# A two-dimensional spectral filter: stage 1 of the first transform in two row tiles of 64 partitions

## The chip, the cores and the metric

The kernel runs on one core of a Trainium2 chip. A core has TensorE (PE, the matrix unit, with its weight loads written as PEld), VectorE (DVE), ScalarE (ACT), GpSimd (POOL) and SyncE (SP), which here only issues transfers, and sixteen DMA engines that all queues share. The metric is the device time of one execution in microseconds. Lower is better.

## The reference

The input x has 2048 rows and 1024 columns in bf16. Two filters, A and B, are applied to the same x, and a gate per row mixes the results:

```
g = sigmoid((x * gate_w).sum(-1, keepdims=True))
a = irfft2(rfft2(x) * (A_w_r + 1j*A_w_i))
b = irfft2(rfft2(x) * (B_w_r + 1j*B_w_i))
out = g * a + (1 - g) * b
```

The filters have 2048 by 513 complex weights each, in bf16. The output is 2048 by 1024 in bf16.

## The kernel before, in words

The transforms are written as matmuls with constant matrices, in seven stages, and the filters' product stands in the middle.

**Stage 1** takes the first part of the transform over the rows. x lies in WB with partition = 4 n1 + 2 b + dh: n1 counts blocks of 64 rows, b says which half of the block a row lies in, and dh is the left or the right half of a row's 1024 columns. The free dimension of WB has 32 rows of 512 columns. They are handled in eight groups c of four rows. The constant M (tile XR) has 64 columns for each of the 32 rows, of which 32 belong to b = 0 and 32 to b = 1; a partition has zeros in the columns of the other half. For each group, `prep` (token pp, line 426) writes a copy with the columns reversed into a zone of XR, `mvariant` (mv, line 417) writes three copies of M with signs, and `stage1` (s1, line 444) makes, for each of two column halves j, a job of eight matmuls: four rows q, once with x and once with the reversed copy, accumulating in PSUM. Each has 128 columns of x as weights and 256 columns of M and its variants as moving data. Group 6 (`FOLDED`) is treated differently: `prep` forms the sum and the difference of x and its reversed copy, and the job has eight matmuls of 128 columns. `evict1` (e1, line 467) copies the PSUM unit into FT. A few matmuls without use (`IDLE`, line 447) stand ahead of two jobs, and eleven of 512 columns at the very start.

**Stage 2** (s2, evicted by e2) takes the transform over the columns, **stage 4** (s4, e4) the second part over the rows. Both come in sixteen units, eight of the columns' set M and eight of set O. POOL swaps real and imaginary parts by transfers from XR to XR (sw). VectorE multiplies with the filters' weights W in tile WA: D with the direct data, S with the swapped ones, each in a quarter q and a half, written for instance D.M.1.1. W comes by `wload` in four groups for set M (("W", "M", 0) to 3) and two for set O (token wo).

**Stage 5** (s5, e5) begins the way back over the rows: 32 units of sixteen matmuls, units 16 to 31 of set M and 0 to 15 of set O. A unit of set O needs all products of that set. **Stages 6 and 7** (s6, e6; s7) end it; ad and cq combine and SP stores the rows.

The **gate** has its own chain: gs and egs take x's spectrum with the gate's weights, `row_sums` (rows) forms partial sums, zp sums them over the partitions on TensorE, ez copies the sums on ScalarE and lets POOL write them to gate_rows in DRAM, and zl lets SP read them back as two broadcasts, the first half of the rows into FT and the second into F2. sg applies the sigmoid on ScalarE (sg.0 the first, sg.1 the second), gm the sign on VectorE, and rb multiplies the result with the constant U5, whose two halves come by the tokens U5 and U5b on SP, behind zl. rb.0 to rb.7 use the first half of U5 and the rows, rb.8 to rb.15 the second. A unit s6.r needs rb.r.

**The order** is written out in `PLAN`, a table of tokens. Each token puts its instructions on its engine in the order of the table, and every engine works in order. The letter or word at the end of a token names the engine (a, d, pe, dma), the number before pe the PSUM unit, of which there are four with two banks each. `Prog` adds the waits that the data need. Transfers on SP go out in the order of the program too: first M and x, then F2 and CK, the W groups of set M with small constants between them, wo.0 and wo.1, the constant tail CL of CK, the gate's broadcasts, U5, DI and U5b, and the stores. A few x transfers are issued by ScalarE.

```
    for c in range(1, 8):
        xload(c, 0, "sp")
        xload(c, 1, "act" if c < 4 else "sp")
```

Of the kernel before, what the change touches and what calls it, by code (L numbers as in the profile page):

```python
# [22 lines left out]
def make_consts():  # L23
# [3 lines left out]
    n1, pb, dh = p // 4, (p // 2) % 2, p % 2  # L27
    M = np.zeros((128, 32, 16, 2, 2))
    for b in range(2):
        on = 1.0 * (pb == b)[:, None]  # L30
        n = 64 * n1[:, None] + 32 * b + np.arange(32)[None, :]
        for t in range(16):
            if t == 0:
                M[:, :, 0, 0, b] = on
                M[:, :, 0, 1, b] = on * ((-1.0) ** n1)[:, None]
            else:
                ph = pi2 * t * n / 2048
                M[:, :, t, 0, b] = on * np.cos(ph)
                M[:, :, t, 1, b] = -on * np.sin(ph)
    C["M"] = M.reshape(128, 2048)  # L40
# [58 lines left out]
    blocks += [np.ones((128, 128))]  # L99
# [60 lines left out]
D.M.0.1..d sw.M.0..dma gw.0.pe s2.M.5.2.pe e4.M.3..a D.M.0.0..d s2.M.4.1.pe egw..a sw.M.1..dma e2.M.5..a  # L160
gs.1.3.pe e2.M.4..a D.M.1.1..d s4.M.5.0.pe egs.1..a s4.M.4.2.pe D.M.1.0..d e4.M.5..a gs.3.1.pe e4.M.4..a
s2.M.7.3.pe S.M.0.1..d egs.3..a s2.O.1.0.pe e2.M.7..a S.M.0.0..d gs.2.2.pe e2.O.1..a S.M.1.1..d s4.M.7.1.pe
sw.M.2..dma egs.2..a s2.M.6.3.pe S.M.1.0..d e4.M.7..a gs.0.0.pe e2.M.6..a D.M.2.1..d s2.O.0.2.pe egs.0..a
D.M.2.0..d s4.M.6.1.pe e2.O.0..a s4.O.1.3.pe rows..d e4.M.6..a s4.O.0.0.pe e4.O.1..a sw.M.3..dma S.M.2.1..d
s2.O.3.2.pe e4.O.0..a s2.O.2.1.pe S.M.2.0..d wo.0..spq e2.O.3..a st.3.pe s2.O.5.0.pe D.O.0.0..d est..a
sw.O.0..dma e2.O.2..a s4.O.3.2.pe D.M.3.0..d e2.O.5..a s4.O.2.3.pe e4.O.3..a D.M.3.1..d s2.O.4.1.pe e4.O.2..a
# [782 lines left out]
```

## Time and profile before

| what | us |
|---|---|
| median of 3 runs | 122.81 (121.64 to 122.82) |
| the profiled execution | 122.8 |
| its span, from the first to the last instruction | 121.0 |
| TensorE busy | 113.5 |
| ScalarE busy | 103.5 |
| VectorE busy | 85.8 |
| GpSimd busy | 17.3 |

The times further down are from the profiled execution and count from the start of its span. In the views a line number such as L463 is a line of the kernel; L326, L329 and L332 are the helpers for transfers and copies, so their groups are told apart by their tiles. L601 is stage 5, L494 stage 2, L509 stage 4, L539 the products, L708 stage 6, L732 stage 7. "SPq" is a transfer being issued by SP; the time until its data land stands in another view. Matmuls overlap in their records, so the cost of one in a row is read from the length of a run of them.

### The profile page before, as it was taken

The numbers are of one execution on the slowest core, as the hardware profiler recorded it, in microseconds if no ns is written. First come the engines' busy times: TensorE is split into PE (matmuls) and PEld (weight loads), VectorE is DVE, ScalarE is ACT, GpSimd is POOL, SyncE is SP. The second block draws the span as 40 slices with busy tenths as digits, with TensorE's granted clock in tenths as the row PEclk, the third lists the DMA queues.
The fourth block names the chain that finished last, engine by engine and source line by source line (L and its number), as shares of the span: only waits on it lengthen the run. The fifth ranks groups of instructions, "written<-read, shape, count | busy, mean of one in ns | idle before, by whom it ended". The sixth has DMA issues, their size and how long they took to land.

```text
span 121.0 us, 3622 instructions
## 1 busy us (share of the span) xinstructions
PE 113.5 (94%) x1546; PEld 99.1 (82%) x1546; DVE 85.8 (71%) x127; ACT 103.5 (86%) x127; POOL 17.3 (14%) x37
## 2 busy tenths in 40 slices
PE   6979999999999999789999989999899999999990
PEld 2358899969689787488799989999899989999980
DVE  0375667319679969999979917999503879787772
ACT  0498999699878999979999989999979688988861
POOL 4000009306003393030530000000000000000000
PEclk9999999999999999999999999999999999999998
DMA  2999999999999999649893999300000334443344
GB/s 61 296 331 370 348 360 332 321 319 344 371 350 325 353 306 256 185 108 277 152 371 117 297 381 418 122 0 5 0 0 5 126 134 173 176 175 119 146 175 173
DMA packets 27519, 26.87 MB, mean 222 GB/s; under 512 B 10208, under 2 KB 23216, under 8 KB 27248
## 3 DMA queue, kind: packets, MB, share of 16 engines
q1 hardware_dynamic: 24368, 20.85, 55.8%
q0 software_dynamic: 1760, 4.49, 10.2%
q10 hardware_dynamic: 1376, 1.31, 3.5%
q8 instruction: 12, 0.20, 0.7%
q14 instruction: 3, 0.02, 0.1%
HBM read 18.23 MB, written 4.20 MB: 185 GB/s over the span
## 4 chain that ended last, share of the span: by engine, by line
PE 42%; DVE 17%; DMA 16%; ACT 12%; issue 5%; SPq 4%; POOL 0%; DVEq 0%; ACTq 0%; POOLq 0%
PE PS L732 11%; PE PS L708 10%; PE PS L463 10%; DMA XR<-XR 10%; ACT WB L329 9%; DVE WA L539 9%; DVE WB L539 5%; PE PS L601 5%; SPq L326 4%; DMA WA<-in_B_w_i_dram 4%; PE PS L494 3%; DMA SM<-c_SM 3%; ACT XR L329 2%; ACT WA L329 2%; DVE WA L776 1%
## 5 line engine op out<-in xcount | busy, mean ns | idle before, releaser
L601 PE MATMUL PS<-CK,WA 128*128 128x128 bf16 x256 | 31.8, 223 | 1.6 <-DVE WA L539 1.6
L601 PEld LDWEIGHTS PS<-CK,WA 128*128 128x128 bf16 x256 | 31.3, 145 | 1.9 <-DVE WA L539 1.9
L329 ACT ACTIVATE XR<-PS 128x1024 bf16<-128x1024 f32 x31 | 29.5, 1035 | 2.9 <-PE PS L494 1.6
L329 ACT ACTIVATE WB<-PS 128x1024 bf16<-128x1024 f32 (+1 forms) x31 | 30.8, 1040 | 1.4 <-PE PS L601 1.2
L601 PE MATMUL PS<-CK,WB 128*128 128x128 bf16 x256 | 31.9, 226 | 0.0
L601 PEld LDWEIGHTS PS<-CK,WB 128*128 128x128 bf16 x256 | 31.3, 145 | 0.1
L329 ACT ACTIVATE WA<-PS 128x1024 bf16<-128x1024 f32 (+5 forms) x34 | 25.3, 807 | 5.5 <-PE PS L708 2.8
L776 DVE TENSOR_TENSOR WA<-PS,WA 128x512 bf16<-128x512 f32 (+1 forms) x30 | 19.7, 711 | 10.7 <-ACT WA L329 10.5
L539 DVE TENSOR_TENSOR WB<-XR,WA 128x2048 bf16<-128x2048 bf16 x16 | 19.1, 1222 | 3.3 <-ACT XR L329 2.6
L539 DVE TENSOR_TENSOR WA<-XR,WA 128x2048 bf16<-128x2048 bf16 x16 | 18.7, 1224 | 2.9 <-DMA XR<-XR 2.8
L732 PE MATMUL PS<-FT,WA 128*128 128x256 bf16 x140 | 17.6, 273 | 0.2 <-ACT WA L329 0.2
L494 PE MATMUL PS<-F,FT 128*128 128x128 bf16 x256 | 16.0, 219 | 0.0
L494 PEld LDWEIGHTS PS<-F,FT 128*128 128x128 bf16 x256 | 14.8, 98 | 0.9
L509 PE MATMUL PS<-XR,CK 128*128 128x512 bf16 (+1 forms) x72 | 15.3, 355 | 0.0
L732 PEld LDWEIGHTS PS<-FT,WA 128*128 128x128 bf16 x140 | 13.1, 98 | 1.6 <-ACT WA L329 0.4
L708 PE MATMUL PS<-XR,WB 128*128 128x128 bf16 x208 | 13.6, 219 | 0.5 <-ACT WB L329 0.4
L708 PEld LDWEIGHTS PS<-XR,WB 128*128 128x128 bf16 x208 | 12.5, 98 | 1.0 <-ACT WB L329 0.8
L329 ACT ACTIVATE FT<-PS 128x1024 bf16<-128x1024 f32 (+1 forms) x14 | 12.4, 988 | 0.3 <-PE PS L463 0.3
L326 POOL DMA_DIRECT2D XR<-XR x16 | 8.4, 529 | 25.1 <-DVE WA L539 12.5
L509 PEld LDWEIGHTS PS<-XR,CK 128*128 128x128 bf16 x72 | 6.5, 97 | 5.1 <-ACT XR L329 0.2
L463 PE MATMUL PS<-XR,WB 128*128 128x256 bf16 x56 | 8.4, 273 | 0.9 <-DMA WB<-in_A_x_dram 0.6
L463 PE MATMUL PS<-XR 128*128 128x256 bf16 x56 | 8.4, 273 | 0.2 <-DVE XR L332 0.2
(74 smaller groups left out, 88.1 us busy)
## 6 DMA issues: line engine op xcount, KB each, us to landing
XR<-XR POOLq DMA_DIRECT2D x16, 256.0 KB, 4.9
out_dram<-WA SPq DMA_DIRECT2D x15, 256.0 KB, 2.0
WB<-in_A_x_dram SPq DMA_DIRECT2D x12, 256.0 KB, 6.9
FT<-c_U SPq DMA_DIRECT2D x2, 1024.0 KB, 9.6
WA<-in_A_w_r_dram SPq DMA_DIRECT2D x7, 192.5 KB, 4.9
WA<-in_A_w_i_dram SPq DMA_DIRECT2D x7, 192.5 KB, 5.0
WA<-in_B_w_r_dram SPq DMA_DIRECT2D x7, 192.5 KB, 5.0
WA<-in_B_w_i_dram SPq DMA_DIRECT2D x7, 192.5 KB, 5.9
```

What stands on the lines that cost most here:

```text
L326: return P.add(eng, lambda e: e.dma_start(dst, src), dma=name, **kw)
L329: return P.add("act", lambda e: e.activation(dst, src, ACT.Copy), **kw)
L463: P.add("pe", lambda e, o=ps(u * 1024 + q * 256, [(1, 256)]), lh=lh, rh=rh, s=s, q=q: e.matmul(o, lh, rh, start=(s == 0 and q % 2 == 0), s ...
L494: P.add("pe", lambda e, o=o, lh=fblock(cmb, j, t), j=j, rh=rh, cmb=cmb: e.matmul(o, lh, rh, start=(j == 0 and cmb == 0), stop=(j == 1), sk ...
L509: P.add("pe", lambda e, o=o, fb=FB[kind, pm, m], m=m, rh=rh: e.matmul(o, sl(CK, fb, [(1, 128)]), rh, start=(m == 0), stop=(m == 1)), r=["C ...
L539: pop[st, q, sw, half] = P.add("dve", lambda e: e.tensor_tensor(out=o, in0=x, in1=w, op=ALU.mult), r=xr(o_, 2048) + wk, a=[("prod", st, sw ...
L601: P.add("pe", lambda e, o=o, lh=sl(t, to + l0, [(hp, 128)]), ab=ab: e.matmul(o, lh, KI(ab), start=(ab == 0), stop=(ab == 1)), r=[("prod", ...
L708: P.add("pe", lambda e, o=o, lh=lh, rh=rh, cp=cp: e.matmul(o, lh, rh, start=(cp == 0), stop=(cp == 1)), r=[("Z", pi), ("RB", r)], w=[("ps" ...
L732: P.add("pe", lambda e, lh=lh, rh=rh, st=st, sp=sp: e.matmul(ps(bank * 512 + o, [(1, 256)]), lh, rh, start=st, stop=sp), r=[("Y", r), "DI" ...
L776: P.add("dve", lambda e, s=s, op=op: e.tensor_tensor(out=sl(WA, outc(r) + 512 * s, [(1, n), (2, 256)]), in0=ps(2 * u * 512, [(256, n), (1, ...
```

## The change

Stage 1 computes the same sums with another layout. The partition of x becomes 64 b + 2 n1 + dh, so each row half b has 64 neighbouring partitions. M loses the zeros and half of its columns. A job now has sixteen matmuls, each on 64 partitions and 128 moving columns; the two row halves write two different banks of the unit. No group is folded. M comes in three pieces instead of four, and `mvariant` works on a whole piece. x comes in seven pieces of four rows (one of eight), each by four transfers to 32 partitions, 28 in all instead of 16 to 64 partitions; five are issued by ScalarE and 23 by SP. FT's layout between stages 1 and 2 changes with it (`evict1`, `fblock`). The zones are eight instead of four. The scratch tile VT of `row_sums` is dropped for the tail of CK, so the transfer CL, which fills that tail, now comes after `row_sums`; a block of ones in CK that nothing reads is dropped. The table `PLAN` is written anew as a whole, so the order of the products, evictions, stage-5 units, rb and the gate's tokens changes too.

```diff
@@ make_consts
-    n1, pb, dh = p // 4, (p // 2) % 2, p % 2
-    M = np.zeros((128, 32, 16, 2, 2))
...
-    C["M"] = M.reshape(128, 2048)
+    n1, pb, dh = p // 2 % 32, p // 64, p % 2
+    M = np.zeros((128, 32, 16, 2))
...
+    C["M"] = M.reshape(128, 1024)
...
-    blocks += [np.ones((128, 128))]
@@ PLAN, the end of stage 1
-pp.5..d e1.4.1..a mv.7.2..d mv.5.3..d e1.4.0..a s1.5.0.2.pe pp.6..d s1.5.1.3.pe e1.5.0..a s1.6.0.0.pe pp.7.0..d
-e1.5.1..a pp.7.1..d s1.7.0.1.pe e1.6.0..d s1.6.1.2.pe e1.7.0.0..a s1.7.1.3.pe e1.7.0.1..d e1.6.1..a
-s2a.M.0.0.pe e1.7.1.1..d e1.7.1.0..a s2a.M.1.1.pe s2b.M.0..pe s2.M.2.2.pe e2.M.0..a s2b.M.1..pe e2.M.2..a
-s4.M.0.3.pe e2.M.1..d s2.M.3.0.pe e4.M.0..a s4.M.1.2.pe e2.M.3..a s4.M.2.1.pe e4.M.1..a s4.M.3.3.pe e4.M.2..a
+s1.4.1.1.pe e1.4.0..a s1.5.1.2.pe pp.6..d s1.6.0.3.pe e1.4.1..d e1.5.1..a s1.6.1.0.pe e1.6.1..a s1.5.0.2.pe
+pp.7.1..d pp.7.0..d e1.6.0..d s1.7.0.1.pe e1.5.0..a s1.7.1.0.pe e1.7.0.1..d e1.7.0.0..a e1.7.1.1..d e1.7.1.0..a
+s2a.M.0.3.pe s2a.M.1.2.pe s2b.M.1..pe s2b.M.0..pe e2.M.1..a s2.M.3.1.pe e2.M.0..d s4.M.1.0.pe e2.M.3..a
+s4.M.0.2.pe e4.M.1..d s2.M.2.3.pe e4.M.0..a s2.M.5.1.pe e2.M.2..a sw.M.0..dma D.M.0.0..d s4.M.3.0.pe e2.M.5..a
+D.M.0.1..d s4.M.2.2.pe e4.M.3..a s4.M.5.3.pe e4.M.2..d s2.M.4.1.pe e4.M.5..a sw.M.1..dma D.M.1.1..d s2.M.6.0.pe
@@ PLAN, from the end of set M in stage 5 to stage 6
-e4.O.7..a sw.O.2..dma s4.O.6.3.pe e5.20..a S.O.1.1..d zp.1.pe s5.26.0.pe e4.O.6..a D.O.2.0..d s5.21.2.pe ez..a
...
-e5.22..a s5.25.2.pe e5.23..a zl..dma S.O.2.1..d U5..dma s5.27.3.pe e5.25..a S.O.2.0..d s5.29.1.pe e5.27..a
-S.O.3.1..d s5.30.0.pe e5.29..a S.O.3.0..d s5.31.2.pe e5.30..a s5.28.3.pe e5.31..a U5b..dma s5.1.1.pe e5.28..a
-s5.11.0.pe e5.1..a s5.5.2.pe e5.11..a s5.12.3.pe sg.0..a e5.5..d ed.1.pe e5.12..a gm.0..d rb.2..d sg.1..a
-s5.13.0.pe rb.1..d rb.3..d eg..a s5.10.2.pe e5.13..d s5.14.3.pe e5.10..a rb.0..d s5.9.1.pe rb.7..d e5.14..a
...
+s5.23.1.pe e5.28..a S.O.2.1..d s5.30.0.pe e5.23..a zp.2.pe s5.31.3.pe S.O.3.0..d e5.30..a s5.27.1.pe ez..a
+S.O.3.1..d e5.31..a e5.27..a s5.7.0.pe s5.13.2.pe e5.7..a s5.11.3.pe e5.13..a zl..dma U5..dma s5.8.1.pe
+e5.11..a s5.15.0.pe e5.8..a s5.4.2.pe e5.15..a s5.12.3.pe e5.4..a s5.1.1.pe sg.1..a e5.12..d U5b..dma ed.0.pe
+e5.1..a gm.1..d sg.0..a s5.9.2.pe eg..a gm.0..d s5.6.3.pe e5.9..d s5.5.1.pe e5.6..a rb.3..d s5.0.0.pe rb.4..d
+e5.5..a rb.9..d s5.10.2.pe e5.0..a rb.6..d rb.7..d s5.2.3.pe e5.10..a rb.5..d s5.14.1.pe rb.0..d e5.2..a
+rb.10..d s5.3.0.pe e5.14..a rb.14..d rb.1..d e5.3..a s6a.0.2.pe rb.8..d s6a.1.3.pe rb.12..d s6b.0..pe s6b.1..pe
...
@@ the loads
-    MP = ((0, 4), (4, 8), (8, 16), (16, 32))
+    MP = ((0, 4), (4, 16), (16, 32))
...
-    def xload(c, dh, eng):
-        src = AP(x2.tensor, x2.offset + 4 * c * 1024 + 512 * dh, [[32 * 1024, 64], [1024, 4], [1, 512]])
-        dma(eng, f"x{c}{dh}", sl(WB, 2048 * c, [(512, 4), (1, 512)], p0=dh, np_=64, pstep=2), src, a=[("x", c)])
+    XP = ((0, 4), (4, 8), (8, 12), (12, 16), (16, 24), (24, 28), (28, 32))
+    def xload(i, b, dh, eng):
+        r, n = XP[i][0], XP[i][1] - XP[i][0]
+        src = AP(x2.tensor, x2.offset + (32 * b + r) * 1024 + 512 * dh, [[64 * 1024, 32], [1024, n], [1, 512]])
+        dma(eng, f"x{i}{eng}", sl(WB, 512 * r, [(512, n), (1, 512)], p0=64 * b + dh, np_=32, pstep=2), src, a=[("x", i)])
...
+    for i in range(7):
+        if i == 0:
+            mload(0, "sp")
+        for dh in range(2):
+            for b in range(2):
+                xload(i, b, dh, "act" if i < 2 and not dh or (i, b, dh) == (2, 0, 0) else "sp")
+        if i in (0, 3):
+            mload(1 + i // 3, "sp")
@@ stage 1
-    IDLE = {(1, 0): 4, (2, 0): 2}
+    IDLE = {(1, 0): 8}
...
-        for s, q in [(s, q) for s in range(2) for q in range(4)] if c not in FOLDED else []:
-            r = 4 * c + q
-            lh = sl(XR, 8192 + 1024 * z + 256 * q + 128 * j, [(1, 128)]) if s else sl(WB, r * 512 + 128 * j, [(1, 128)])
-            rh = sl(XR, 64 * r, [(4096 * s, 2), (2048, 2), (1, 64)])
...
+        for s in range(2):
+            for q in range(4):
+                r = 4 * c + q
+                for b in range(2):
+                    t, o = (XR, 4096 + 1024 * z + 256 * q + 128 * j) if s else (WB, r * 512 + 128 * j)
+                    lh, rh = sl(t, o, [(1, 128)], 64 * b, 64), sl(XR, 32 * r, [(2048 * s, 2), (1024, 2), (1, 32)], 64 * b, 64)
+                    P.add("pe", lambda e, o=ps((2 * u + b) * 512 + q * 128, [(1, 128)]), lh=lh, rh=rh, s=s, q=q: e.matmul(o, lh, rh, start=(s == 0 and q == 0), stop=(s == 1), skip_group_check=True),
...
@@ row_sums
+        VT = sl(CK, 1280, [(1, 1024)]).bitcast(f32)
```

More of the change, by code (lines that the diff above doesn't have):

```diff
@@ L162 @@
[L162 to L166, printed above, removed]
@@ L459, in stage1 @@
[L459 to L464 removed]
+        i = piece(MP, 4 * c)
@@ L465, in stage1 @@
         zones.drop(c, 2)
     def evict1(eng, c, j, u, half=None):
[L468 to L470 removed]
+        o, n = (half, 1) if half is not None else (0, 2)
+        copy(eng, sl(FT, j * 8192 + 4 * c + 32 * o, [(64, 128), (32, n), (1, 4)]), ps((2 * u + o) * 512, [(1, 128), (512, n), (128, 4)]),
+             r=banks(u)[o:o + n], a=[("F1", j)])
@@ L844, in bass_gated_mix__spectral_gfnet__spectral_gfnet__prompt_kernel @@
             if b:
+                assert "rows" in {t.split(".")[0] for t in PLAN.split()[:PLAN.split().index(token)]}
                 dma("sp", "CL", sl(CK, 1280, [(1, NK - 1280)]).bitcast(u16), cst["CK"].ap()[:, 1280:], w=["CL"])
```

129 lines of the change are left out of this document (45 added, 84 removed).

## The prediction

> **What bounds the kernel now.** First the engines' busy time and the chain that ended last (start, length, engine, tile, line), then windows (PE, PEld, DVE, ACT, POOL busy, clock, DMA share, GB/s).
>
> ```profile
> PE 113.5 (94%) x1546; PEld 99.1 (82%) x1546; DVE 85.8 (71%) x127; ACT 103.5 (86%) x127; POOL 17.3 (14%) x37
> ...
> 17.90 0.45 PE PS L457 x8
> ...
> 19.67 0.87 PE PS L463 x8
> 20.54 2.80 PE PS L494 x48
> ...
> 24.24 0.91 PE PS L494 x16
> ...
> 27.94 6.07 DMA XR<-XR
> ...
> 70.01 4.06 PE PS L601 x63
> ...
> 77.51 11.25 ACT WB L329 x11
> ...
> 88.81 2.41 PE PS L708 x40
> ...
> 15.00:16.50 1.50, 1.50 (x16) 1.34 (x15) 0.75 (x3) 1.50 (x3) 0.00 (x0) 1.00 1.11 352
> 34.10:51.80 17.70, 16.53 (x248) 12.98 (x245) 16.72 (x19) 16.55 (x21) 6.31 (x12) 1.00 1.02 285
> 51.80:70.00 18.20, 17.77 (x265) 16.53 (x265) 17.44 (x17) 17.48 (x20) 3.71 (x7) 1.00 0.80 228
> ```
>
> Stage 1 ends and stage 2 begins at 20.54; stage 6 begins at 88.81. TensorE is busy 94% of the span, but not alone: while stage 1 runs, the DMA engines are full too (share 1.11, 352 GB/s), and from 34.1 to 70.0 VectorE works 34.16 of 35.9 us. So TensorE time taken out of stage 1 is a gain only if x, the products' W and the later stages come sooner as well. Next, SP's queue and when its data land (count; min/median/max ns; first and last start; or start and length; last, size and us to landing).
>
> ```profile
> L326 SPq DMA_DIRECT2D out_dram<-WA x16: 332/332/338, 94.2 to 118.4; - x16
> L326 SPq DMA_DIRECT2D WB<-in_A_x_dram x12: 616/618/919, 1.1 to 10.4; - x12
> L326 SPq DMA_DIRECT2D WA<-in_A_w_r_dram x12: 601/617/2102, 12.2 to 54.6; - x12
> ...
> 11.13 0.53 SPq L326 DMA_DIRECT2D F<-c_F  x1
> 17.63 2.10 SPq L326 DMA_DIRECT2D WA<-in_A_w_r_dram  x1
> 23.73 0.62 SPq L326 DMA_DIRECT2D WA<-in_B_w_i_dram  x1
> ...
> WB<-in_A_x_dram SPq DMA_DIRECT2D x1, 256.0 KB, 7.1
> WA<-in_B_w_i_dram SPq DMA_DIRECT2D x1, 192.5 KB, 5.9
> WB<-in_A_x_dram SPq DMA_DIRECT2D x1, 256.0 KB, 4.1
> XR<-c_M SPq DMA_DIRECT2D x1, 64.0 KB, 2.0
> ```
>
> The 7.1 belongs to the last x (issued at 10.4, landed at 17.5), the 5.9 to the last W of the second group (23.73, 29.6), the 4.1 and 2.0 to SP's first x and first M, when the queues were empty. An issue of a flat 128-partition transfer costs 0.33. One of 64 partitions with an inner list of rows costs 0.62, whether that list has 3, 4, 7 or 8 rows (x and W alike): the price goes by the transfer, not by its rows.
>
> **The change, part by part.**
>
> *Matmuls of stage 1.* A job of 8 matmuls of 256 columns costs 0.87 (fourteen jobs; the two of the folded group 0.45). It becomes 16 of 64 partitions and 128 columns. No row tile is in this trace. Bounds: the two halves run side by side, then 8 x 0.057 = 0.45 (0.057 is 0.91 / 16, stage 2's row); or one after the other, 0.91. I take 0.45: the pairs write different banks and read different partitions. All 16 jobs then cost 7.3 instead of 14 x 0.87 + 2 x 0.45 = 13.1, up to 5.8 less, if x keeps up. The idle matmuls shrink from six of 256 columns to eight of 128: nothing.
>
> *M, its variants, the fold.* 0.26 MB less to load, worth 0.75 us at 352 GB/s where the DMA is the bound; fewer and shorter VectorE and ScalarE instructions ahead of stage 1. All of it lies beside the waits for x, so I cost it at nothing. Without that cover it would be a gain below 0.75.
>
> *x by 32 partitions.* SP issues 23 x transfers instead of 12 (ScalarE 5 instead of 4). What one costs is not in the trace: from 0.33 (most have 128 pieces of 1 KB, as many pieces as a flat 128-partition transfer) to 0.62 (it has the shape of the old x and of W). I take 0.62, the nearest row in shape. With 0.04 between issues, 11 x 0.66 = 7.3 us more on SP. The last x is issued at 10.4 + 7.3 = 17.7. At 128 KB per 0.66 (199 GB/s) the queues are by then empty, and landing takes between 2.0 and 4.1; by size 2.7. x is complete at 20.4, not 17.5.
>
> Behind it stand on VectorE, in the new table's order, two reversed copies, a whole eviction (e1.6.0) and a half one; stage 2 needs both evictions.
>
> ```profile
> 17.58 0.49 DVE L332 COPY XR<-WB 128x512 bf16<-128x512 bf16 x2
> 20.58 0.69 DVE L332 CAST FT<-PS 128x512 bf16<-128x512 f32 x1 [0.37 <-PE PS L463]
> 23.38 1.23 DVE L332 CAST XR<-PS 128x1024 bf16<-128x1024 f32 x1 [2.11 <-PE PS L494]
> 34.11 4.66 DVE L539 TENSOR_TENSOR WA<-XR,WA 128x2048 bf16<-128x2048 bf16 x4 [1.92 <-DMA XR<-XR]
> 51.81 0.27 PE L601 MATMUL PS<-CK,WA 128*128 128x128 bf16 x1 [1.18 <-DVE WA L539]
> 70.01 0.27 PE L601 MATMUL PS<-CK,WA 128*128 128x128 bf16 x1 [0.42 <-DVE WA L539]
> ```
>
> 20.4 + 0.49 + 1.23 + 0.69 = 22.8; stage 2 starts at 22.9, 2.35 late. F2, now issued at 11.13 + 7.3 = 18.4, is there. From 20.54 to 70.01 (the first stage-5 unit of set O) TensorE has 49.5 us, 1.18 + 0.42 of them idle: 47.9 of work, which the new table doesn't change. TensorE is ready for set O at 22.9 + 47.9 = 70.8.
>
> *W behind x on SP.* The last W of the second group moves from 23.73 by 7.3, less the 1.48 that one issue at 17.63 took over the usual 0.62 on a full queue: 29.55. Landing between 2.7 and 5.9, say 4.0: 33.5, where 29.6 was. The product D.M.1.1 waits for it. After it and D.M.1.0, S.M.0.1 starts at 33.5 + 2 x 1.17 + 0.08 = 35.9 (before: 34.11). The same 34.16 of VectorE work follows, and one eviction more, e2.O.0 (1.23): set O's products end at 71.3 (70.0 to 73.2 by the landing). Set O thus starts at 71.4, 1.4 late. The three other evictions that the table gives VectorE here (e2.M.0, e4.M.1, e4.M.2) lie in the wait for W. The first swap landed 13.5 after stage 2's start (27.94 + 6.07); it now stands one unit of 0.91 sooner, so 35.5, in time for S.M.0.1. row_sums in CK's tail makes the CL load wait for rows, with six products standing between the two: nothing.
>
> *The gate chain in the new table.* This part is not in stage 1 at all. zp stood eleven stage-5 units before set O's first; now two stand between (31 and 27). Behind it hang ez, the write of gate_rows, its two broadcasts, U5, DI and U5b, in a row on SP, and from them the sixteen rb.
>
> ```profile
> 58.48 0.20 PE L626 MATMUL PS<-ATB,MK 128*64 128x32 bf16 x1
> 59.55 0.18 ACT L329 ACTIVATE AT<-PS 64x32 f32<-64x32 f32 x1
> 60.03 0.56 POOL L326 DMA_DIRECT2D gate_rows<-AT  x1 [0.73 <-ACT AT L329]
> 65.47 0.33 SPq L326 DMA_DIRECT2D FT<-gate_rows  x1
> 67.73 0.34 SPq L326 DMA_DIRECT2D FT<-c_U  x1
> 73.07 1.14 ACT L645 ACTIVATE FT<-FT,SM 128x1024 bf16<-128x1024 f32 x1
> 74.89 1.90 DVE L657 TENSOR_TENSOR XR<-FT 128x1024 bf16<-128x1024 bf16 x3
> ...
> gate_rows<-AT POOLq DMA_DIRECT2D x1, 8.0 KB, 5.4
> SM<-c_SM POOLq DMA_DIRECT2D x1, 2.5 KB, 3.4
> FT<-c_U SPq DMA_DIRECT2D x1, 1024.0 KB, 10.9
> F<-gate_rows SPq DMA_DIRECT2D x1, 512.0 KB, 5.2
> ```
>
> Before, U5b landed at 67.73 + 10.9 = 78.6 and stage 6 had 10 us in hand. Now zp runs two units (2 x 16 x 4.06 / 63 = 2.06) before 70.8, at 68.7, and ez 1.07 later, at 69.8. The write is issued 0.48 on. Its landing took 5.4 among the swaps and W; now these are done, so I take the 3.4 of POOL's small load at the start, with 2.0 and 5.4 as ends. The broadcasts start at 73.7, 8.2 late, and U5b lands at 86.8. Third in the new order stands rb.9, which reads U5b; from it to rb.1, without which s6a.1 can't run, are eight of 0.63: 91.9. Ahead of s6a.1 there is 0.45 of s6a.0, so stage 6 runs as if begun at 91.4: **2.6 late**. ScalarE allows some 90: six evictions of 1.02 from 72.6, sg.1 at 79.3 when its broadcast has landed (73.7 + 0.45 + 5.2), then two sg of 1.14 and eight evictions.
>
> **Sum.** Stages 6 and 7 keep their work, so the span is 121.0 + 2.6 = 123.6. The profiled execution took 122.8, 1.8 over its span, and the median shown is 122.81: 125.4. The write's ends move it to 124.0 (2.0; ScalarE then near 90.0) and 127.4 (5.4).
>
> [...]
>
> ```profile
> 1.20 3.98 PE L379 MATMUL PS<-F 128*128 128x512 bf16 x11 [1.20 <-DVE SM L381]
> ```
>
> Eleven matmuls of 512 columns took 3.98, 0.36 each; by stage 1's 0.109 for 256 columns they would take 0.22. So TensorE begins slow. With x at 199 GB/s, stage 1's 7.3 us of jobs would lie in 15 us, and TensorE would idle for half of them. [...]
>
> **Rivals.**
>
> *Short issues (faster).* If a 32-partition transfer costs 0.33, SP is done with x as early as before, and the DMA bound moves it to 17.5 - 0.75 = 16.8. Stage 2 starts at 19.3, TensorE is ready for set O at 67.2; W lands at 28.9, S.M.0.1 follows at 31.3 and products end at 66.8. zp then runs 3.6 sooner than in my forecast: stage 6 begins at 87.8, or 86.4 with the write at 2.0: 121.8 or 120.3, 121.1 in the middle. For it: as many pieces as a flat transfer. Against: the issues of 3 and of 8 rows cost alike. It decides below some 0.45 an issue. 17%.
>
> *Half price (no change).* At 0.47 an issue, 23 x 0.51 against 12 x 0.66 is 3.8 more on SP; data still bind x (17.0), stage 2 starts at 19.5, zp at 65.3, U5b lands at 83.4, rb.1 ends at 88.4: stage 6 as if at 88.0, 122.0. 21%.
>
> *No pairs: the row tiles don't do what they are for.* Jobs of 0.91 change only the last two behind x, at most 0.5, hidden behind e1.6.0 on VectorE: 125.4 to 125.9, inside the forecast.
>
> [...]
>
> *One half at a time.* If a transfer to 64 neighbouring partitions got only half of 352, 128 KB would take 0.74, against 0.66 of issue; 4.19 MB end at 2.6 + 23.8 = 26.4, stage 2 6 us later than forecast, 131. For it, nothing in this trace; against it, that ScalarE's and SP's transfers, and successive ones, alternate between the halves. 5%. [...]
>
> **How the numbers follow.** Forecast 48% (124.0 to 127.4), short issues 17%, half price 21%, slow clock 9%, half ports 5%. The range leaves out half of the fast case and the tails above: 121.3 to 127.6. One per cent (121.6 and 124.0), about what can be told from no change here, splits the cases: faster 16%, within 22% (half price and a little of the rest), slower 62%.
>
> **What the profile after would show.** Issues of 32x4x512 near 0.62 on SP, F2 issued at 18 or later, x complete near 20, TensorE idle between the pieces; stage-1 matmuls starting in pairs; D.M.1.1 waiting for W; gate_rows broadcast after set O's first unit; rb.9 waiting for U5b, and stage 6 for VectorE. If F2 is issued by 12, or U5b has landed by 80, the forecast is wrong at that step.

## The result, and the profile after

The changed kernel took 127.33 us (median of 4 runs, 126.87 to 127.68) against 122.81 for the kernel before: a ratio of 1.0386, with a 95% interval of 1.0309 to 1.0464. It is slower, by 4.5 us. In this document a median is over all runs of a kernel, while a ratio leaves out runs that came out over 1.5% above the fastest of the same kernel, so the two can differ a little. The profiled execution took 127.0 us with a span of 125.2 us, 4.2 us over the span before.

Two lines of the profile's page for the changed kernel: the engines' busy time, and the granted TensorE clock in 40 slices. In its views L430 is the matmuls without use, L439 stage 1, L470 stage 2, L515 the products, L579 stage 5, L635 rb, L686 stage 6; L316, L319 and L322 are the helpers for transfers and copies.

```profile
PE 110.5 (88%) x1676; PEld 96.2 (77%) x1676; DVE 89.9 (72%) x123; ACT 96.6 (77%) x117; POOL 17.4 (14%) x37
PEclk9999955999999999999999999999999999999998
```

TensorE has 3.0 us less to do and ScalarE 6.9 us less, as the change meant, and the kernel is longer all the same. The clock fell to half in the sixth and seventh slice. The chain of the changed kernel between 14 and 30 us, and its piece ahead of stage 6 (start, length, what), say where the time went:

```profile
16.66 0.61 SPq L316
...
17.31 5.34 DMA WB<-in_A_x_dram
...
22.67 0.30 DVE XR L322
...
23.00 0.29 DVE XR L322
23.29 1.74 DVE FT L322 x2
...
25.25 2.84 PE PS L470 x48
...
85.87 7.43 ACT WB L319 x7
...
93.35 1.96 PE PS L686 x32
```

Stage 1 no longer hangs on TensorE but on SP's issues, then on the landing of the last x, then on VectorE's copies and evictions. Stage 2 begins at 25.25 where it began at 20.54: 4.7 late, and the span is 4.2 longer. Stage 6 begins at 93.35, behind seven of ScalarE's evictions and not behind VectorE. What SP paid and when (first the group of the x issues: min/median/max ns, first and last start; then its timeline), from the changed kernel:

```profile
L316 SPq DMA_DIRECT2D WB<-in_A_x_dram x23: 592/605/1045, 1.1 to 17.3; - x23
...
18.03 0.52 SPq L316 DMA_DIRECT2D F<-c_F  x1
...
29.44 0.62 SPq L316 DMA_DIRECT2D WA<-in_B_w_i_dram  x1
```

And what the DMA did meanwhile (busy time of PE, PEld, DVE, ACT, POOL; clock, DMA share, GB/s):

```profile
12.00:18.00 6.00, 1.24 (x32) 0.90 (x32) 2.27 (x5) 3.05 (x4) 0.00 (x0) 0.76 1.14 234
...
16.50:18.00 1.50, 0.00 (x0) 0.00 (x0) 0.00 (x0) 0.00 (x0) 0.00 (x0) 0.50 1.13 256
...
22.50:24.00 1.50, 1.44 (x46) 1.09 (x42) 1.30 (x3) 1.32 (x3) 0.72 (x2) 1.00 1.14 339
```

This is the surprise. The 16 DMA engines are as full as before (share 1.09 to 1.17 in windows of 1.5 us between 9 and 21 us, against 1.11), but they move 221 to 277 GB/s where they moved 352. While x is landing, TensorE stands still from 13.96 to 18.68. Later, the lines that answer the prediction's steps (VectorE's timeline, then TensorE's with two half jobs first):

```profile
34.80 1.24 DVE L515 TENSOR_TENSOR WB<-XR,WA 128x2048 bf16<-128x2048 bf16 x1 [0.17 <-DMA WA<-in_B_w_i_dram]
37.36 2.38 DVE L515 TENSOR_TENSOR WA<-XR,WA 128x2048 bf16<-128x2048 bf16 x2
86.09 4.89 DVE L635 TENSOR_TENSOR XR<-FT 128x1024 bf16<-128x1024 bf16 x8
...
13.35 0.39 PE L439 MATMUL PS<-XR,WB 64*128 64x128 bf16 x8
13.57 0.39 PE L439 MATMUL PS<-XR 64*128 64x128 bf16 x8
...
74.51 0.27 PE L579 MATMUL PS<-CK,WA 128*128 128x128 bf16 x1 [1.32 <-DVE WA L515]
```

### The profile page after: what moved, and what is told of

Read it like the earlier page. It is cut to its first block, busy times and chain, and to the rows that moved or that the text cites. A ratio compares the mean times of both kernels' runs of the same rounds, so it can differ in the third digit from the quotient of the medians.

```text
span 125.2 us, 3874 instructions
## 1 busy us (share of the span) xinstructions
PE 110.5 (88%) x1676; PEld 96.2 (77%) x1676; DVE 89.9 (72%) x123; ACT 96.6 (77%) x117; POOL 17.4 (14%) x37
## 4 chain that ended last, share of the span: by engine, by line
PE 43%; DVE 23%; SPq 12%; DMA 9%; ACT 6%; issue 4%; DVEq 0%
SPq L316 12%; PE PS L710 11%; PE PS L686 11%; DVE WA L515 9%; DVE WB L515 8%; PE PS L579 8%; PE PS L470 7%; ACT WB L319 6%; PE PS L485 6%; DMA XR<-XR 5%; DMA WB<-in_A_x_dram 4%; DVE FT L322 1%; DVE XR L322 1%; PE PS L664 1%; DVE WA L754 1%
## 5 line engine op out<-in xcount | busy, mean ns | idle before, releaser
L579 PE MATMUL PS<-CK,WA 128*128 128x128 bf16 x256 | 31.7, 223 | 1.3 <-DVE WA L515 1.3
L579 PEld LDWEIGHTS PS<-CK,WA 128*128 128x128 bf16 x256 | 31.2, 145 | 1.7 <-DVE WA L515 1.5
L579 PE MATMUL PS<-CK,WB 128*128 128x128 bf16 x256 | 31.8, 225 | 0.0
L319 ACT ACTIVATE WB<-PS 128x1024 bf16<-128x1024 f32 (+1 forms) x31 | 30.3, 1062 | 1.7 <-PE PS L579 1.5
L579 PEld LDWEIGHTS PS<-CK,WB 128*128 128x128 bf16 x256 | 31.3, 145 | 0.4
L319 ACT ACTIVATE XR<-PS 128x1024 bf16<-128x1024 f32 x28 | 26.7, 1041 | 4.1 <-PE PS L470 1.8
L319 ACT ACTIVATE WA<-PS 128x1024 bf16<-128x1024 f32 (+5 forms) x34 | 25.4, 804 | 5.0 <-PE PS L686 3.9
L515 DVE TENSOR_TENSOR WA<-XR,WA 128x2048 bf16<-128x2048 bf16 x16 | 18.9, 1226 | 1.2 <-DMA XR<-XR 1.1
L515 DVE TENSOR_TENSOR WB<-XR,WA 128x2048 bf16<-128x2048 bf16 x16 | 19.1, 1223 | 0.9 <-ACT XR L319 0.7
L470 PE MATMUL PS<-F,FT 128*128 128x128 bf16 x256 | 15.6, 219 | 0.8 <-DVE FT L322 0.8
L470 PEld LDWEIGHTS PS<-F,FT 128*128 128x128 bf16 x256 | 14.7, 98 | 1.9 <-DVE FT L322 1.0
L319 ACT ACTIVATE FT<-PS 128x1024 bf16<-128x1024 f32 (+1 forms) x11 | 9.9, 945 | 7.6 <-PE PS L439 7.6
L686 PE MATMUL PS<-XR,WB 128*128 128x128 bf16 x208 | 13.6, 219 | 0.6 <-ACT WB L319 0.6
L439 PE MATMUL PS<-XR,WB 64*128 64x128 bf16 x128 | 7.2, 240 | 7.3 <-DMA WB<-in_A_x_dram 7.1
L686 PEld LDWEIGHTS PS<-XR,WB 128*128 128x128 bf16 x208 | 12.5, 98 | 1.1 <-ACT WB L319 0.9
L316 POOL DMA_DIRECT2D XR<-XR x16 | 8.4, 529 | 25.9 <-DVE WA L515 12.5
L439 PEld LDWEIGHTS PS<-XR,WB 64*128 64x128 bf16 x128 | 4.8, 106 | 8.7 <-DMA WB<-in_A_x_dram 6.4
```

The lines of the kernel that those rows point to most:

```text
L316: return P.add(eng, lambda e: e.dma_start(dst, src), dma=name, **kw)
L319: return P.add("act", lambda e: e.activation(dst, src, ACT.Copy), **kw)
L439: P.add("pe", lambda e, o=ps((2 * u + b) * 512 + q * 128, [(1, 128)]), lh=lh, rh=rh, s=s, q=q: e.matmul(o, lh, rh, start=(s == 0 and q == ...
L470: P.add("pe", lambda e, o=o, lh=fblock(cmb, j, t), j=j, rh=rh, cmb=cmb: e.matmul(o, lh, rh, start=(j == 0 and cmb == 0), stop=(j == 1), sk ...
L515: pop[st, q, sw, half] = P.add("dve", lambda e: e.tensor_tensor(out=o, in0=x, in1=w, op=ALU.mult), r=xr(o_, 2048) + wk, a=[("prod", st, sw ...
L579: P.add("pe", lambda e, o=o, lh=sl(t, to + l0, [(hp, 128)]), ab=ab: e.matmul(o, lh, KI(ab), start=(ab == 0), stop=(ab == 1)), r=[("prod", ...
```

## The experiments

Two things about the loads of x could cost: **the price per transfer on SP** (28 transfers in place of 16), and **the rate of a transfer that reaches only one half of the partitions**. Beside them stand the clock, the gate's place in the new table, and the order of W. The text of each expectation was written before its run; all ratios are to the kernel before, timed beside the run.

### The rate: where the partitions lie, and where the rows come from

e1_spread changes the destination only; e2_pitch changes the source only.

```diff
-p0=64 * b + dh, np_=32, pstep=2
+p0=2 * b + dh, np_=32, pstep=4                                   # e1_spread
-x2.offset + (32 * b + r) * 1024 + 512 * dh, [[64 * 1024, 32], ...
+x2.offset + (1024 * b + r) * 1024 + 512 * dh, [[32 * 1024, 32], ... # e2_pitch
```

> The changed kernel, with each x transfer written to 32 partitions four apart over all 128 (p = 4 n1 + 2 b + dh) instead of two apart within one half. Source, sizes, order and issues stay; x then lies in other rows than M expects, so the output is another sum. Half-port theory (a transfer within 64 neighbouring partitions is slower to write): the DMA share falls below 1 while x loads, the last x, issued at 17.3, lands by 20.4 instead of 22.65, stage 2 starts near 23 instead of 25.25, and the time is 124.5 to 125.5. Source-pitch theory (rows read 128 KB apart are slow) and issue theory: x lands at 22.6 as before this edit, 127.3.

> The changed kernel, with each x transfer read from rows 64 KB apart (row 32 n1 + 1024 b + r, each row still read once) instead of 128 KB apart. Destinations, sizes, order and issues stay; other rows stand in the partitions, so the output is another sum. Source-pitch theory: x lands by 20.4, stage 2 near 23, 124.5 to 125.5. Half-port theory and issue theory: unchanged, x at 22.6, 127.3.

Measured: e1_spread 127.9 us, ratio 1.0456 (1.0379 to 1.0533); e2_pitch 127.75 us, 1.0429 (1.031 to 1.0549). The one execution of e1_spread that was profiled ran at a mean clock of 0.66 and took 162 us, so only its DMA is read here. Windows of e1_spread, then of e2_pitch:

```profile
12.00:18.00 6.00, 3.02 (x64) 2.37 (x62) 2.74 (x6) 3.22 (x5) 0.00 (x0) 0.62 0.84 261
```

```profile
12.00:18.00 6.00, 1.41 (x38) 0.90 (x32) 2.51 (x5) 3.38 (x4) 0.00 (x0) 0.85 1.14 233
```

The source pitch did nothing: 1.14 and 233 GB/s are as good as the changed kernel's own numbers (1.14 and 234). That idea falls. Spread over all partitions, the same bytes kept the engines only 0.84 busy: per byte, an engine was held for some two thirds of the time (0.84 at 261 against 1.14 at 233). So here the destination made the DMA full. Yet the time did not fall: it came out where the theory of issues had it and not at 124.5 to 125.5, so this was not the whole of it. The same pair was run again with TensorE kept busy (below), where both profiles can be compared.

### The price of an issue alone

e4_before_32 is the kernel *before*, with its matmuls, table and fold, whose transfers of x are cut into two of 32 partitions, spread over all 128.

```diff
+for b in range(2):
-    src = ...4 * c * 1024 + 512 * dh, [[32 * 1024, 64], [1024, 4], [1, 512]]   ... p0=dh, np_=64, pstep=2
+    src = ...(32 * b + 4 * c) * 1024 + 512 * dh, [[64 * 1024, 32], [1024, 4], [1, 512]] ... p0=2 * b + dh, np_=32, pstep=4
```

> The kernel before, with each x transfer cut in two of 32 partitions (four apart over all 128, source rows 128 KB apart), so SP has 12 issues more and ScalarE 4. Nothing else changes. Issue theory: SP's F2 is issued near 18.5 to 19, the last x lands near 20.5, stage 2 starts 2.5 to 3 later, 124.5 to 126. Half-port theory adds nothing here (DMA share below 1 at the end of x). Source-pitch theory: x at 250 GB/s, landing at 21.5 or later, 126 or more. If the issues of 32 partitions were free, 122.8.

Measured: 128.4 us, ratio 1.048 (1.0387 to 1.0574). SP's group of x issues and two windows of e4_before_32:

```profile
L326 SPq DMA_DIRECT2D WB<-in_A_x_dram x24: 598/605/774, 1.1 to 17.5; - x24
```

```profile
15.00:18.00 3.00, 3.00 (x30) 2.61 (x29) 0.99 (x5) 3.00 (x5) 0.00 (x0) 1.00 0.70 191
18.00:21.00 3.00, 1.10 (x13) 0.63 (x10) 1.39 (x2) 2.70 (x3) 0.00 (x0) 1.00 0.65 185
```

Here the DMA is not full (0.65 to 0.70) and moves 185 to 191 GB/s, because no more is handed to it (SP hands over 128 KB for each issue of 0.605 us); the last x landed at 21.26 and stage 2 began at 25.11. No row tile, no new table and no half: the count of issues, with the waits that it brings, is enough for a loss as large as the change's. It is more than the 124.5 to 126 expected. Part of the difference is the clock: it was at 0.50 from 21.9 to 25.4 us, behind TensorE's waits, and the last 24 matmuls of stage 1 took 3.84 us (21.27 to 25.11), where the kernel before, at 1.00, takes 2.2 (two jobs of 0.87 and one of 0.45).

### Fewer issues, halves kept

e3_two_queues hands all transfers of the second half to ScalarE's queue. e5_big leaves the queues and makes 20 transfers of the 28 (M's last piece moves up with them).

```diff
-"act" if i < 2 and not dh or (i, b, dh) == (2, 0, 0) else "sp"
+"act" if b else "sp"                                             # e3_two_queues
-XP = ((0, 4), (4, 8), (8, 12), (12, 16), (16, 24), (24, 28), (28, 32))
+XP = ((0, 4), (4, 8), (8, 16), (16, 24), (24, 32))               # e5_big
```

> The changed kernel, with all 14 x transfers of half b = 0 issued by SP and all 14 of b = 1 by ScalarE, so the two halves are in flight together and SP has 9 issues fewer. Half-port theory together with the issue price: SP is done with x near 11.5, x moves at 300 to 350 GB/s and lands at 15.5 to 17.5, stage 2 starts at 18.5 to 20, set O by 69, and the gate chain is then the next bound: 122 to 123.5. Source-pitch theory: x stays at 250 GB/s and lands at 20 to 21, 125.

> The changed kernel, with x in five pieces of 4, 4, 8, 8 and 8 rows instead of seven: 20 transfers instead of 28, 15 of them on SP instead of 23; M's last piece moves up with them. Issue theory alone: SP issues F2 near 12.8 instead of 18.0, x moves at 350 GB/s and lands at 16 to 17, stage 2 starts at 18.5 to 19.5, 121.5 to 122.5. Half-port theory: the DMA engines stay full at 250 to 280 GB/s, x lands at 18.5 to 20.5, stage 2 starts at 21 to 23, 123 to 125.5.

Measured: e3_two_queues 127.79 us, ratio 1.0376 (1.0271 to 1.0481); e5_big 132.38 us, 1.0818 (1.0745 to 1.0891). In e3_two_queues SP was free for stage 2's constants at 12.18, 5.85 sooner than in the changed kernel, and the time is no better. Expected, if the halves in flight together added up, were 300 to 350 GB/s and 122 to 123.5 us; with both queues at work the window was this:

```profile
9.00:12.00 3.00, 0.00 (x0) 0.00 (x0) 1.21 (x3) 1.58 (x3) 0.00 (x0) 1.00 1.10 286
```

The run has a cost of its own, since ScalarE issued until 10.4 and made its first eviction only at 12.3. In e5_big stage 2's constants were issued at 14.05, and it is the slowest of all, where both theories had it at 125.5 or less. Its window and its chain:

```profile
12.00:18.00 6.00, 3.65 (x64) 3.28 (x64) 3.50 (x6) 3.26 (x5) 0.00 (x0) 0.50 1.14 222
```

```profile
12.03 12.20 DMA WB<-in_A_x_dram
...
28.17 3.18 PE PS L470 x48
```

SP was done with x at 12.0, but the last x landed 12.2 us later: the DMA was full at 222 GB/s, and W, issued from 15.65 us on, shared that rate. Behind the last x stood five jobs of stage 1 (its last pieces have 8 rows), three of them at half the clock, and stage 2 began 3.9 us after it. With the issues out of the way the halves are thus enough for the loss as well; how much of this run's loss is theirs, e9_spread_big below tells. With the last x issued sooner (12.0 us against 17.3), the wait only moved from its queue into the DMA's (12.2 us to land against 5.34).

### The clock, and the rate again

e6_warm puts 80 matmuls without use ahead of job 4; e7_spread_warm adds the destination of e1_spread.

```diff
-IDLE = {(1, 0): 8}
+IDLE = {(1, 0): 8, (4, 0): 80}
```

> The changed kernel, with 80 more idle matmuls of 128 columns ahead of the job that waits for x's rows 16 to 23, so that TensorE is busy from 14 to 18.5 and its clock stays up. Nothing else. By the trace of the changed kernel the low clock (15 to 21.7) lies wholly in waits for x, and stage 2 runs at full rate: 126.5 to 127.5, no change against 127.33. Slow-clock theory: 1.5 us of stage 2 come back, 125 to 126.

> The same idle matmuls, and each x transfer written to 32 partitions four apart over all 128, as in e1_spread (x lies in other rows than M expects, so the output is another sum). With the clock held up the price of the half ports stands alone. Half-port theory: DMA share below 0.9 while x loads, x lands 1 us sooner than in e6_warm, stage 2 starts 1 us sooner, and the time is 0.7 to 1.3 below e6_warm's. Issue theory alone: the same time as e6_warm.

Measured: e6_warm 128.18 us, ratio 1.0491 (1.0438 to 1.0544); e7_spread_warm 128.41 us, 1.0475 (1.0398 to 1.0553). Filling the wait bought nothing, as expected; the mean clock of e6_warm's four runs ranged from 0.971 to 1.000, and their times lie within 0.5 us. So here the half clock is a sign of the wait for x, not a cost of its own. For e7_spread_warm 0.7 to 1.3 us less than e6_warm was expected, and there was no gain. The pair shows the halves' price. VectorE's copy of the last x in e6_warm, then the same in e7_spread_warm with what followed (the bracket is the idle time ahead and what ended it):

```profile
23.32 0.62 DVE L322 COPY XR<-WB 128x512 bf16<-128x512 bf16 x2 [0.59 <-DMA WB<-in_A_x_dram]
```

```profile
20.42 0.62 DVE L322 COPY XR<-WB 128x512 bf16<-128x512 bf16 x2 [0.52 <-DMA WB<-in_A_x_dram]
...
22.83 2.85 PE L470 MATMUL PS<-F,FT 128*128 128x128 bf16 x48 [0.89 <-DVE FT L322]
...
29.99 0.65 SPq L316 DMA_DIRECT2D WA<-in_B_w_i_dram  x1
...
37.91 1.25 DVE L515 TENSOR_TENSOR WB<-XR,WA 128x2048 bf16<-128x2048 bf16 x1 [5.20 <-DMA WA<-in_B_w_i_dram]
```

With the same issues, spreading brings the last x 2.9 us sooner and stage 2 from 25.74 to 22.83. Both are the prediction's own numbers (20.4 and 22.9). But VectorE then waits 5.20 us for the last W of the second group, issued at 29.99 behind all the x and landing 7.8 later (5.2 in the changed kernel; why it took longer stays open), and the gain is gone. This is the likely reason why e1_spread was no faster: **two costs of the same size stand side by side**, and taking away either one alone shows the other.

### The gate in the new table

e8_gate_early moves zp eight and ez ten stage-5 units ahead in the table.

```diff
-sw.O.2..dma e5.17..a s5.20.2.pe ... e5.23..a zp.2.pe s5.31.3.pe ... s5.27.1.pe ez..a
+sw.O.2..dma e5.17..a zp.2.pe ez..a s5.20.2.pe ... e5.23..a s5.31.3.pe ... s5.27.1.pe
```

> The changed kernel, with zp and ez ten stage-5 units earlier in the table (ahead of unit 20 instead of behind unit 30); all else in place. The prediction's gate step: U5b lands sooner and stage 6 starts 1.6 sooner, 125.7. By the trace of the changed kernel, where the write of gate_rows landed in 1.7 and set O's evictions on ScalarE ended last, nothing or up to 0.5: 126.8 to 127.5.

Measured: 128.42 us, ratio 1.051 (1.0439 to 1.058), e6_warm beside it 1.0491. The gate's rows were written from 66.99 and U5b was issued at 72.72, where the changed kernel had 72.36 and 75.90. In this execution the last x landed at 24.25 and stage 2 began at 27.11, 1.9 later than in the changed kernel's, so stage 6 is set against stage 2: it began 67.9 us behind it (at 94.99), where the changed kernel took 68.1. That is no gain to speak of, and the time is above the 126.8 to 127.5 expected. With x this late the gate's chain has room; ScalarE's seven evictions end last ahead of stage 6.

### Both costs away

e9_spread_big joins e5_big and e1_spread. e11_small_tail cuts its last rows into 12 and 4 and keeps TensorE warm.

```diff
-XP = ((0, 4), (4, 8), (8, 12), (12, 16), (16, 24), (24, 28), (28, 32))
+XP = ((0, 4), (4, 8), (8, 16), (16, 24), (24, 32))               # e9_spread_big
+XP = ((0, 4), (4, 8), (8, 16), (16, 28), (28, 32))               # e11_small_tail
+IDLE = {(1, 0): 8, (4, 0): 20, (7, 0): 20}                       # e11_small_tail
 p0=2 * b + dh, np_=32, pstep=4                                   # both
```

> The changed kernel with x in 20 transfers instead of 28 (five pieces, the later ones of 8 rows) and with each transfer's 32 partitions spread over all 128 (every fourth), so that both halves of the partitions take part in each; the matmuls then add up other rows, so the output is another sum. This takes away the two costs together: e7_spread_warm took away the half-partition rate alone and lost 2.9 us of gain to W, which was issued as late as before; e5_big took away issues alone and had its transfers slower. If the rate of half the partitions and SP's issue queue are the whole of the loss: constants of stage 2 issued at about 14, the last x landed by 18.5 to 19.5, stage 2 begun at 20.5 to 21.5, no wait of several us for W, and a time of 121.5 to 124 (near the kernel before, where x landed at 17.8 and stage 2 began at 20.54). If the row tiles or the new job table cost something after stage 2 by themselves, stage 2 begins early and the time stays at 125 or over. If the rate isn't a matter of the partitions, x lands at 24 as in e5_big and the time is 132.

> e9_spread_big with the last 16 rows of x cut into 12 and 4 in place of 8 and 8, so that only one job of matmuls is left when the last piece lands, and with 20 matmuls without use ahead of jobs 4 and 7, so that the TensorE is not cold then; as there, the transfers are spread over all partitions and the output is another sum. In e9 the last x landed at 19.1, then five half jobs ran at a granted clock of 0.50 and stage 2 began at 23.64, 3.1 later than in the kernel before, for a ratio of 1.0254. If the whole of the loss stands ahead of stage 2, the last x again lands at 18.5 to 19.5, stage 2 begins at 21.3 to 22.3 at a granted clock of 1.00, and the time is 122.5 to 124.2, a ratio of 1.005 to 1.016. If something behind stage 2 (W, the new job table) costs by itself, stage 2 begins early and the ratio stays at 1.02 or over, as it did in e7_spread_warm.

Measured: e9_spread_big 125.59 us, ratio 1.0254 (1.0167 to 1.034); e11_small_tail 125.71 us, 1.026 (1.0168 to 1.0351). Windows of e9_spread_big, then its chain from 70 us on, then two pieces of e11_small_tail's chain:

```profile
12.00:18.00 6.00, 3.43 (x104) 2.77 (x99) 3.61 (x7) 5.40 (x6) 0.00 (x0) 1.00 1.07 352
...
20.00:21.00 1.00, 1.00 (x24) 1.00 (x22) 0.97 (x3) 0.00 (x0) 1.00 (x3) 0.50 1.11 327
```

```profile
75.93 10.82 DMA FT<-c_U
...
86.78 3.70 DVE XR L635 x6
...
91.74 1.29 PE PS L686 x20
```

```profile
20.17 1.22 PE PS L430 x20
...
74.76 12.49 DMA FT<-c_U
```

Set against e5_big, which differs by the destination alone, the rate between 12 and 18 is 352 in place of 222 GB/s and the time 6.8 us less. That is the clearest sight of the halves. Against the kernel before, some 2.5% is still missing, and both my numbers for these runs were too good. In e9_spread_big the last x landed at 19.11 (as expected), but five jobs were left, at a clock of 0.50, and stage 2 began at 23.64 instead of 20.5 to 21.5. In e11_small_tail stage 2 began at 22.77, of which my own 20 matmuls took 1.22 on the path. And that 0.9 us did not reach the end: in both, the chain now runs through U5b, which landed at 86.75 and 87.25, and the rb behind it. What is late next is the gate's place in the new table. With the gate ahead, as in e8_gate_early, this was not tried, so what is left then stays open.

### Do two queues fill both halves?

e10_three_queues loads half 0 from SP and half 1 from GpSimd at once, beside ScalarE's five transfers, and lets W wait for the fifth piece of x.

```diff
-"act" if ... else "sp"
+"act" if ... else "pool" if b else "sp"
-wload("sp", ("W", "M", 0), 0, 4, (0,), 0, 385, 0)
+wload("sp", ("W", "M", 0), 0, 4, (0,), 0, 385, 0, [("x", 4)])
```

> The changed kernel with its 28 transfers of x as they are, 32 partitions of one half each, but issued from three queues: ScalarE's five as now, of the others those of half 0 from SP and those of half 1 from GpSimd, so that both halves are loaded side by side; W waits for the fifth piece of x, so that it does not take the rate. If what hurts is that one queue hands out one half at a time, the rate in 10 to 18 us goes from 221 to 277 GB/s to over 300, the last x lands at 18 to 19.5, stage 2 begins at 21 to 22 and the time is 121 to 124. [...]

Measured: 131.01 us, ratio 1.0717 (1.0633 to 1.08). GpSimd had issued its twelve by 8.8 and SP its last x by 11.3. Windows of e10_three_queues:

```profile
12.00:15.00 3.00, 1.29 (x40) 0.94 (x36) 1.32 (x2) 2.05 (x3) 0.00 (x0) 1.00 1.05 227
15.00:18.00 3.00, 0.44 (x16) 0.27 (x10) 1.69 (x3) 1.63 (x2) 0.00 (x0) 1.00 1.08 252
18.00:21.00 3.00, 0.19 (x5) 0.20 (x7) 0.21 (x1) 0.00 (x0) 0.00 (x0) 0.50 1.16 194
```

Everything was in the queues, both halves at once, no W beside it from 12.4 to 20.8, and the full DMA moved 194 to 252 GB/s. Halves one after the other (222 in e5_big) and halves side by side both stayed below the 352 of transfers over all 128 partitions (e9_spread_big, 12 to 18 us). GpSimd's queue could be slower by itself, which this run can't tell; but e3_two_queues, with SP and ScalarE, moved 286 GB/s between 9 and 12 us, where e9_spread_big moved 364.

### A half or a quarter

e12_quarters gives each transfer 32 neighbouring partitions instead of every second one of 64.

```diff
-p0=64 * b + dh, np_=32, pstep=2
+p0=64 * b + 32 * dh, np_=32
```

> The changed kernel with the 32 partitions of each transfer of x next to each other, one quarter of the partitions, in place of every second one of a half; the same 28 transfers, queues and bytes; the matmuls then add up other rows, so the output is another sum. The three queues of e10 fed both halves side by side and the rate stayed at 194 to 277 GB/s, so that a port of each half, idle while the other half is written, is no longer a sufficient reason. If what counts is how many groups of neighbouring partitions one transfer is spread over, a quarter is slower than a half: a rate of 130 to 210 GB/s at a full DMA share between 12 and 21 us, the last x at 25 to 33, a time of 130 to 138. If only the half counts, the rate stays at 221 to 277, the last x lands at 22 to 23.5 and the time is 127 to 128.5.

Measured: 128.07 us, ratio 1.0443 (1.0339 to 1.0547). SP's group of x issues, and windows of e12_quarters:

```profile
L316 SPq DMA_DIRECT2D WB<-in_A_x_dram x23: 425/432/456, 1.1 to 12.6; - x23
```

```profile
12.00:15.00 3.00, 1.24 (x32) 0.90 (x32) 2.12 (x4) 2.45 (x3) 0.00 (x0) 1.00 1.14 216
15.00:18.00 3.00, 0.84 (x16) 0.72 (x18) 0.76 (x2) 0.00 (x0) 0.00 (x0) 0.77 1.14 245
```

The quarter went at the rate of the half (231 GB/s between 12 and 18 us, 234 in the changed kernel), so how much of the half a transfer touches made no difference here. By accident the run also cut the issue to 0.43 us and let SP finish x 4.7 us sooner; the last x still landed at 22.21, where it was 22.65. It confirms e3_two_queues and e5_big: while the halves bound, a cheaper issue was worth nothing. What makes a half slower than the whole, no run shows.

### One table

Of each profiled execution but e1_spread's: where x was complete for VectorE, where stage 2 began, and the rest of the span.

| kernel | last x | stage 2 | span | span after stage 2's start |
|---|---|---|---|---|
| before | 17.5 | 20.54 | 121.0 | 100.5 |
| after | 22.65 | 25.25 | 125.2 | 100.0 |
| e2_pitch | 22.53 | 25.47 | 125.5 | 100.0 |
| e3_two_queues | by 22.0 | 24.42 | 126.5 | 102.1 |
| e4_before_32 | 21.26 | 25.11 | 125.1 | 100.0 |
| e5_big | 24.25 | 28.17 | 130.1 | 101.9 |
| e6_warm | 23.32 | 25.74 | 126.7 | 101.0 |
| e7_spread_warm | 20.42 | 22.83 | 126.5 | 103.7 |
| e8_gate_early | 24.25 | 27.11 | 126.8 | 99.7 |
| e9_spread_big | 19.11 | 23.64 | 124.0 | 100.4 |
| e10_three_queues | by 23.9 | 27.71 | 128.5 | 100.8 |
| e11_small_tail | by 19.2 | 22.77 | 124.5 | 101.7 |
| e12_quarters | 22.21 | 24.62 | 126.6 | 102.0 |

The rest of the span stays within 99.7 and 102.1 us in all but e7_spread_warm, where W was late. So the changed kernel's loss stands ahead of stage 2. Behind it the changed kernel is half a microsecond shorter than the one before, which is no more than its runs differ among themselves (spans of 125.1 to 125.9). No version that beats the kernel before was found.

## Why the prediction was right, and where it was wrong

The sign and the range were right: 125.4 was forecast, 127.33 came, inside 121.3 to 127.6 and near its upper end. The path was not the one forecast: 2.6 us were to come through the gate, and the 4.2 of the span came through x, stage 2 and ScalarE's evictions. That the number fell into the range is partly luck.

**Issues: right.** 0.62 was taken for a transfer of 32 partitions; the median was 0.605. The last x was issued at 17.31 (forecast 17.7), F2 at 18.03 (18.4). The rivals of short issues and of half price are out. The reason given was only half right: the price does not go by the transfer alone, for e12_quarters paid 0.43 for as many partitions and rows next to each other.

**Landing of x: the step that failed.** The prediction said that at 128 KB per 0.66 (199 GB/s) the queues would be empty by the last issue, and took 2.7 us for the landing. It was 5.34, with the DMA full. Two things were mis-sized in that one line. First the demand: four of SP's 23 transfers are of 256 KB, and ScalarE's five and M come on top, so 4.45 MB (x 4.19, M 0.26) were handed over by 17.9. The DMA was hardly busy before 2.6 (share 0.13); to move all of it by 17.9 it would have needed 291 GB/s, and it moved 243. Second the supply: transfers to one half got 221 to 277 GB/s, not 352. I had priced this rival ("one half at a time") at 5%; it was largely what happened, short of the 131 us given for it, because the measured rate lies above the 176 GB/s (half of 352) that I took, by estimate, for one half. The reason against it, that transfers alternate between the halves, fell in e3_two_queues and e10_three_queues.

**Stage 2: structure right, time late.** Behind x stood the two copies and the evictions that were named, 2.6 us long; 22.65 + 2.6 = 25.25 instead of 22.9, 2.35 more than forecast.

**Row tiles: right.** Two runs of eight matmuls of a job start 0.22 apart (13.35 and 13.57) and a job takes 0.45 to 0.46, so the pairs run side by side. It bought nothing, since TensorE waited for x.

**W: its landing was mis-sized too, but hardly felt in this kernel.** The last W was issued at 29.44 (forecast 29.55) and landed after 5.2 instead of 4.0; an eviction that x had delayed stood ahead of D.M.1.1, so VectorE waited only 0.17 us for W. The products D.M.1.1 and S.M.0.1 began at 34.80 and 37.36 (forecast 33.5 and 35.9). From there to the end of set O's products VectorE took 37.1 us where the sum had 35.4; among its waits are 0.75 for TensorE and 1.08 for a swap. Set O began at 74.51, forecast 71.4. In e7_spread_warm, with x as early as forecast, W landed after 7.8 and set O began at 75.55. So the landing of x alone would not have saved the forecast's path.

**Gate chain: named, but it cost nothing in this kernel.** Forecast were 2.6 us from it, 1.2 of them beyond set O's 1.4. U5b did land when forecast (75.90 + 10.8 = 86.7, forecast 86.8), by luck: the write of gate_rows was issued at 72.36 instead of 70.3 and landed in 1.7 instead of 3.4. But the rb began at 86.09 and ran eight in a row without a wait, and stage 6 began at 93.35, 18.8 after set O's first unit as in the kernel before. x's further 2.35 us had moved everything else behind the chain: one error made up for the other. Where x and W both came early, the chain did bind: e11_small_tail had stage 2 at 22.77, U5b at 87.25 (forecast 86.8), a wait for it, and stage 6 at 92.24 (forecast 91.4). In e7_spread_warm, with x as early but W late, it did not: ScalarE's evictions ended last again, and stage 6 began at 94.36.

**Clock: it fell, but not in stage 2.** It was at 0.50 from 15.15 to 21.98 us. The fall came 1.2 us after TensorE's last matmul and 3.5 us ahead of the next, in the wait for x. The rival given 9%, three us of stage 2 at half the rate, was my estimate, which no row of the kernel before shows; in the changed kernel the clock was back at 1.00 there, and by e6_warm (four runs within 0.5 us at mean clocks of 0.971 to 1.000) the fall cost nothing in this kernel. It did cost where jobs of stage 1 were still to run behind the last x, as in e4_before_32 and e9_spread_big.

## What to carry to other kernels

Halving the partitions of a transfer cost twice here: SP paid 0.605 us for each of 23 transfers where it had paid 0.618 for each of 12, and transfers that stay within one half of the partitions moved bytes at some two thirds of the rate (222 against 352 GB/s between e5_big and e9_spread_big) with the DMA as busy (share 1.14 against 1.07). So a matmul that wants its operand in two halves should be weighed by its loads first; and read GB/s beside the DMA share, since here a full share at a lower rate was a slower transfer, not more work. When two costs of one size lie side by side, taking away either can show nothing, as in e1_spread (127.9 us) and e5_big (132.38); take away both before calling one of them harmless.

## What the runs showed of the hardware

- Transfers within one half of the partitions kept the 16 DMA engines full (share 1.13 to 1.15) at 207 GB/s (e5_big, 12 to 15 us) to 256 (the changed kernel, 16.5 to 18) in the windows with little but x, whether they took every second partition of the half or a quarter in a row; from three queues at once it was 194 to 252 (e10_three_queues), from two 286 (e3_two_queues); spread over all 128 they reached 352 at 1.07 (e9_spread_big).
- An issue on SP took 0.605 us with every second (the changed kernel) or fourth partition (e4_before_32), and 0.43 with neighbouring ones (e12_quarters), for the same 32 partitions and 4 to 8 rows.
- The granted clock stood at 0.50 for 6.8 us in the changed kernel (15.15 to 21.98). By the mean clock of windows of 3 us it was 3.4 us in e6_warm, e9_spread_big and e12_quarters, and 10.3 us in e8_gate_early, where it ended at 25.9 though work had begun again at 20.03.
- The fall came 1.2 us after the last matmul in the changed kernel, by the same windows 0.1 us after it in e5_big and 3.2 us after it in e12_quarters, and in e6_warm while matmuls ran (at 13.5). What sets its moment and its length, these runs do not show.
- The write of the gate's 8 KB landed in 1.7 us on a quiet DMA (share 0.03 between 72.0 and 74.2), where it took 5.4 in the kernel before, beside the swaps and W.
